# Sliding-window attention with sink keys feeding an MLP, on one core: the first four blocks' queries and keys read in 2,048-byte pieces, the sink values loaded early, a new written order

## The chip, the cores and the metric

The kernel runs on one core of one Trainium2 chip. The metric is the time of one execution in device microseconds (us); the kernel before was run three times. Engines are named as the profile names them: PE (matrix products), PEld (its weight loads), DVE (vector), ACT (activations), POOL, SP (both also start transfers; "POOLq" and "SPq" are their queues). PE reads from the on-chip working memory and writes to a small accumulator memory (PSUM), from which DVE and ACT copy results out.

## The reference

Two stages. Attention with batch 4, 8 heads, 768 positions and head size 64, where a query sees the last 128 positions and the first 4 (the sinks); then, per token, a two-layer MLP (512 to 2,048 to 512).

```python
scores = scale * np.matmul(q, k.transpose(0, 1, 3, 2))
is_sink = pos[None, :] < int(n_sink)                 # n_sink = 4
in_window = (rel >= 0) & (rel < int(window))         # window = 128, rel = query - key
scores = np.where(is_sink | in_window, scores, -1000000000.0)
a = softmax(scores); attn = a @ v
x = attn.transpose(0, 2, 1, 3).reshape(3072, 512)
h = x @ w_in                                         # 512 x 2048
out = (h * (1.0 / (1.0 + np.exp(-1.702 * h)))) @ w_out   # 2048 x 512
```

## The kernel before, in words

The 3,072 tokens are 24 blocks of 128 (six per batch). `ORDER` puts the four first blocks of the batches in front (0, 6, 12, 18): these see only themselves, so they need neither a previous block nor sinks. Two neighbouring places of `ORDER` form a group; the MLP runs over 12 groups of 256 tokens.

Per block: the queries, keys and values are loaded by POOL's queue with a cast from float32 to float16 (`load_block`, L273 for q and k, L254 for v). One load, the keys of the very first block, goes through SP's queue as float32 (`raw_k`, L261) and is cast by DVE (L269). Each of these loads puts a token on a partition and reads its 8 heads, that is, 128 x 8 pieces of 64 numbers, 256 bytes each. For the first eight blocks PE turns q and k (features onto partitions): four 128x128 transposes for q and four for k (L379, tile `tq`), copied to `qkT` by DVE or ACT (L344, L348). For later blocks a transposing transfer on SP does this (L401). Then scores `own` (and `prv` against the previous block, L449; `snk` against the sink keys, L478), a mask by DVE (L495), maximum (L505) and subtraction (L546), exponential on ACT (L585), transposition of the weights (by PE, L625, tile `ta`, for six blocks; by SP's queue, `at<-a`, for the rest), two selects on POOL (L588, L592), the product with v (`av`, L677 to L687), normalisation on DVE (L694, L695), a transposition (`tx`, L713, or SP's queue), and the MLP: `hT` = w_in by x (L748), the gate (ACT, L778; for the first group tanh on ACT, L762, and a product on DVE, L769), and `o` = gate by w_out (L802), copied to `osb` and stored.

The sink values take a path of their own. `vsa` is set to ones by DVE (L232), 4 rows of v per batch are loaded into it on SP (L318), a mask `ownm` is loaded on SP (L227), and POOL or DVE multiplies them into `vsb` (L323), which `av` reads for every block that has sinks (L677).

The order is written out: `SEQUENCE` lists all 834 steps with the engine that each is put on (`s` SP, `d` DVE, `t` POOL, `p` PE, `a` ACT), and each engine works through its own steps in this order. A step that waits holds up all that stands behind it on its engine. Numbers that the text uses: 0 is the load of the constants, 37 the `raw_k` load, 5 the setting of `vsa`, 93 to 96 the sink values' loads, 97 to 100 the `vsb` products, 21 to 26 the loads of w_in and v. The costs in `plan.add` served the search for the order; at run time they do nothing. Rings of buffers (`RING`) bound what may run ahead: three general PSUM tiles (`mm`), one `mi`, one `own`, one `pv`. POOL has at most eight loads under way: each further one waits for the load eight places before it.

Of the kernel before, what the change touches and what calls it, by code (L numbers as in the profile page):

```python
# [11 lines left out]
FP32 = mybir.dt.float32  # L12
# [7 lines left out]
P = 128  # L20
D = 64
# [16 lines left out]
    tanh=(0, 1),  # L38
    last=(256, 128, 128),
    hw=["k0"],  # L40
    avb={0: ("mi", "mm"), 1: ("mi", "mm"), 2: ("mi", "mm")},
    hb={},
    tqb={0: ("mm", "mi"), 1: ("mm", "mi")},
# [15 lines left out]
172p 21t 9d 7d 153p 134d 173a 30t 133d 136a 116p 29t 154d 175p 117a 156d 118p 24t 135a 139p 120p 158a 121d 137p 34t  # L59
138a 119d 140a 33t 155d 122p 176p 123a 157d 141p 143p 160p 142d 481p 159a 27t 144d 161a 177d 482a 145p 164p 484p  # L60
146a 483d 179d 485a 487p 28t 178d 486d 493p 488a 180d 162p 494a 489d 32t 163a 165d 490p 181a 495d 40t 166p 491a 478p
167d 128t 182a 492d 183p 479a 184d 36t 195p 480d 187p 185p 39t 193p 188d 499p 194a 186d 42t 189p 496p 500a 190d 105t
196a 501d 497a 168p 31t 198p 197p 169a 498d 215p 151t 191p 199d 217p 192a 514p 43t 218a 200d 502p 216a 515a 518p 48t
201d 203d 503p 202d 519a 508p 204a 49t 219p 509p 221d 35t 239p 510p 222d 240a 220p 504p 223d 44t 511p 224d 174t 505p
512a 225d 226a 45t 237p 520p 238d 5d 506a 93s 205p 241p 521a 206d 1s 242p 516p 243d 207t 530p 517a 244d 46t 524p 50t
245d 253p 525a 255p 531p 97t 254d 246d 256a 208p 52t 532p 247d 209d 54t 227p 257p 228a 522p 210t 259d 258p 230p 270s
533p 229t 260d 231a 523a 211p 261d 232t 528p 263d 212d 526p 529a 57t 262d 233p 527a 41t 536p 264a 234d 65t 537p 534d
55t 213p 271p 51t 214d 248a 235p 273d 538p 236a 249s 272p 539p 274d 548p 540a 265s 275d 556p 276d 549a 550p 296s
283p 557a 542p 285d 250t 551a 94s 552p 507s 543a 277d 286d 96s 544p 535s 61t 554p 545a 266t 553a 251p 555a 546p 252d
284p 564p 547a 287d 60t 278a 267p 288d 58t 565p 289d 47t 268d 558p 290a 100t 98d 269s 297p 559p 299d 279s 298p 560p  # L70
300d 566p 291s 301d 561p 303d 302d 322s 567p 562a 578p 304a 568d 280t 309p 579a 305s 580p 311d 310p 576p 563s 312d
292t 513s 572p 577a 581a 281p 570p 282d 67t 574p 313d 571a 53t 314d 293p 575a 66t 584p 573a 294d 306t 586p 585a 315d
295s 316a 582p 587p 70t 592p 62t 583a 317s 307p 56t 593p 308d 64t 588p 69t 323p 63t 598p 325d 72t 324p 594p 599a
326d 73t 589p 59t 327d 602p 590a 329d 328d 318t 595p 604p 596a 335p 605a 612p 337d 600p 613a 603a 348s 319p 606p
320d 608p 338d 607a 321s 601a 336p 610p 609a 339d 541s 330a 614p 341d 340d 615p 620p 342a 331s 621p 611a 616p 343s
361p 622p 597s 363d 374s 632p 364d 623p 633a 332t 362p 628p 365d 624d 617p 629a 366d 634p 75t 618a 636p 344t 619s
635a 349p 630p 351d 638p 84t 631a 367d 352d 345p 76t 639a 626p 79t 346d 350p 640p 71t 627a 353d 637a 333p 355d 78t
354d 641a 648p 68t 334d 356a 649p 347s 642p 375p 95s 368a 643p 377d 569s 376p 650p 357s 378d 644p 369s 379d 651p
380d 668p 591s 99t 400s 652d 645p 669a 85t 381d 656p 646d 358t 387p 647s 657a 664p 389d 666p 370t 390d 388p 662p
667a 391d 359p 663a 91t 658p 360d 81t 654p 393d 659a 392d 82t 665a 371p 655a 660p 74t 372d 670p 661a 373s 382a 401p  # L80
676p 403d 402p 671p 404d 394a 383s 677p 405d 672p 407d 395s 406d 678p 625s 673p 408a 413p 674a 409s 679p 415d 384t
684p 426s 680d 690p 685a 416d 696p 396t 385p 691a 688p 697a 386d 77t 414p 692p 689a 417d 87t 397p 418d 693a 682p 80t
419d 398d 686p 410t 683a 399s 698p 687a 420a 699p 88t 411p 86t 694p 412d 83t 421s 700p 695a 90t 427p 724p 429d 712p
725a 430d 428p 716p 713a 431d 720p 717a 432d 710p 433d 439p 711a 701p 721a 441d 422t 718p 702d 452s 704p 719a 442d
714p 653s 423p 715a 440p 434a 732p 424d 705p 443d 425s 444d 733p 435s 722p 445d 446a 706p 723a 447s 734p 707p 703s
675s 465p 708d 744p 467d 436t 752p 745a 468d 735p 753a 750p 92t 736a 437p 448t 751a 466p 740p 469d 438d 748p 741a
89t 471d 449p 470d 749a 738p 450d 746p 451s 453p 747a 726p 455d 742p 456d 454p 727p 743a 739a 457d 728p 472a 459d
458d 760p 729p 761p 460a 730d 772p 731s 473s 762p 773a 763p 709s 461s 770p 764a 774p 771a 768p 474t 775a 776p 769a
766p 777a 462t 780p 767a 778p 788p 779a 781a 475p 789p 476d 782p 463p 754p 464d 783p 477s 755p 681s 784p 785p 756p
786a 790p 787s 802p 791p 803a 757p 792a 794p 804p 758a 795a 759s 808p 805a 793s 796p 737s 809a 765s 800p 797a 806p  # L90
801a 798p 807a 810p 799a 822p 811p 823p 812p 816p 813p 824p 814a 817p 825p 818p 815s 826d 828p 827s 819p 829p 820d
830p 831p 821s 832a 833a
"""


# [69 lines left out]
def kernel(  # L165
# [50 lines left out]


    def hw(key, cost, fn, xfer, **kw):
        return plan.add(SP, key, cost, fn, xfer=xfer, post=1.3, **kw)

    def by(e):
        return nc.sync if e == SP else nc.scalar
# [26 lines left out]
    def load_block(which, b, key, after=0.0):  # L249
        bb, r = divmod(b, 6)  # L250
        pair, i = divmod(PLACE[b], 2)
        src = {"q": q, "k": k, "v": v}[which][bb, :, r * P : (r + 1) * P, :].rearrange("h s d -> s h d")
        if which == "v":
            return sw(key, 0.88, lambda b=b, x=2: nc.gpsimd.dma_start(v65[:, b, :, 0:D], src), 0.93 if pair < 4 else 1.05, deps=[z_1], after=after)  # L254
        w = "qk".index(which)
        buf = qkn[pair]
        if which + str(PLACE[b]) in CFG["hw"]:
            raw = const.tile([P, H, D], FP32, name=f"raw_{which}{b}")
            n = CFG["hw"].index(which + str(PLACE[b]))
            got = plan.add(  # L260
                {SP: 0.45, ACT: 0.6}, -120 + n, 0, lambda e, src=src, raw=raw, x=9: by(e).dma_start(raw, src), xfer=1.2, post=0.6  # L261
            )

            def round16(e, b=b, w=w, i=i):
                dst, src = buf()[:, i, w], raw
# [94 lines left out]
    for p, b in enumerate(ORDER):  # L360
# [8 lines left out]
        if p in CFG["tq"]:  # L369
            tps = [ps(t, (P, 4, P), FP16, f"tq{b}_{w}") for w, t in enumerate(CFG["tqb"][p])] if p in CFG["tqb"] else []  # L370
            tps = tps or [ps("mm", (P, 8, P), FP16, f"tq{b}")] * 2

            def tp(w, tps=tps):
                return tps[w]()[:, 4 * w : 4 * w + 4] if tps[0] is tps[1] else tps[w]()

            def t_qk(w, g=g, i=i, tp=tp):
                src = qkn[g]()[:, i, w].rearrange("p h d -> p (h d)")
                for c in range(4):
                    nc.tensor.transpose(tp(w)[:, c], src[:, bass.ts(c, P)], ident)  # L379

            def copy_qk(e, w, b=b, p=p, tp=tp):
                copy(e, qk_of(b)[:, 4 * w : 4 * w + 4], tp(w))

            parts = []
            for w in range(2):
                a = plan.add(
                    PE, K0 - 48 + w, 0.24, lambda w=w, f=t_qk: f(w), deps=[ld["qk"[w] + str(b)], o_const],
                    take=[tps[w]], give=[qkn[g]],
                )
                parts.append(  # L390
                    plan.add(
                        {DVE: 0.34, ACT: 0.5}, K0 - 48 + w, 0,
                        lambda e, b=b, w=w, f=copy_qk: f(e, w),
                        deps=[a], take=[qkt[g]], give=[tps[w]],
                    )
                )
            o_qkt[b] = parts
        elif i == 0:

            def t_qk(g=g):  # L400
# [3 lines left out]

            o_qkt[b] = o_qkt[ORDER[p + 1]] = [
                plan.add(
                    SP, K0 - 48, 1.4, t_qk, deps=[ld[f"{w}{n}"] for w in "qk" for n in ORDER[p : p + 2]], take=[qkt[g]],
                    give=[qkn[g]], xfer=2.56, post=0.75,
                )
            ]  # L410
# [452 lines left out]
```

## Time and profile before

| | |
|---|---|
| median of three runs | 229.97 us (229.97 to 230.83) |
| the profiled execution: its own time | 231.84 us |
| its span, first to last instruction | 230.1 us |
| busy: PE, DVE, ACT, POOL | 215.8, 132.7, 130.5, 117.5 us |
| first MLP product (`hT`) starts at | 19.33 us |
| last PE instruction ends at about | 227 us |
| pieces moved by POOL's queue | 78,064 |

The profile shows one execution. A row of a table by windows gives, for a stretch of the span, each engine's busy time and its count of instructions, the granted clock, the share of the 16 transfer engines (it can pass 1 where transfers overlap) and GB/s, counted at the destination. A row of a list of waits gives the waiting engine and line, what ended the wait, the total, how often, and the longest. A row of the timeline gives start, length, engine, line, what is written from what, and in brackets how long the engine stood idle before it and what ended that.

### The profile page before, as it was taken

The numbers are of one execution on the slowest core, as the hardware profiler recorded it, in microseconds if no ns is written. First come the engines' busy times: TensorE is split into PE (matmuls) and PEld (weight loads), VectorE is DVE, ScalarE is ACT, GpSimd is POOL, SyncE is SP. The second block draws the span as 40 slices with busy tenths as digits, with TensorE's granted clock in tenths as the row PEclk, the third lists the DMA queues.
The fourth block names the chain that finished last, engine by engine and source line by source line (L and its number), as shares of the span: only waits on it lengthen the run. The fifth ranks groups of instructions, "written<-read, shape, count | busy, mean of one in ns | idle before, by whom it ended". The sixth has DMA issues, their size and how long they took to land.

```text
span 230.1 us, 5428 instructions
## 1 busy us (share of the span) xinstructions
PE 215.8 (94%) x2282; PEld 151.8 (66%) x2282; DVE 132.7 (58%) x236; ACT 130.5 (57%) x188; POOL 117.5 (51%) x138
## 2 busy tenths in 40 slices
PE   1796899998999999999999999999999999999994
PEld 0555785777685586576686586596866865855864
DVE  3579887778858863556566877672873672030001
ACT  2388679644867268247558338659555538512621
POOL 8974574569639279950493573497213700700000
PEclk9999999999999999999999999999999999999999
DMA  9999999999999999999999899899999544304402
GB/s 114 146 178 206 168 207 187 154 74 140 96 147 201 169 179 169 124 140 165 240 142 132 180 169 161 181 162 126 114 124 238 37 59 106 90 3 137 182 3 91
DMA packets 130680, 32.47 MB, mean 141 GB/s; under 512 B 123072, under 2 KB 127712, under 8 KB 130656
## 3 DMA queue, kind: packets, MB, share of 16 engines
q0 software_dynamic: 78064, 13.51, 82.0%
q1 hardware_dynamic: 52448, 18.55, 42.4%
q8 instruction: 18, 0.29, 0.5%
q10 hardware_dynamic: 144, 0.07, 0.1%
q14 instruction: 6, 0.05, 0.1%
HBM read 27.46 MB, written 6.29 MB: 147 GB/s over the span
## 4 chain that ended last, share of the span: by engine, by line
PE 69%; DMA 14%; POOL 12%; SPq 1%; issue 1%; DVE 1%; ACT 1%; POOLq 0%
PE o L802 30%; PE hT L748 28%; DMA w_in<-in_moe_w_in_dram 5%; POOL qkn L273 5%; DMA at<-a 5%; DMA v<-in_v_dram 2%; PE own L449 2%; DMA ownm<-cown 2%; PE av L683 2%; POOL atp L588 2%; POOL at L592 2%; PE av L687 2%; POOL v L254 2%; PE prv L449 1%; PE av L677 1%; SPq L650 1%
## 5 line engine op out<-in xcount | busy, mean ns | idle before, releaser
L748 PE MATMUL hT<-xT,w_in 128*128 128x256 f16 (+1 forms) x896 | 93.6, 257 | 1.7 <-DMA w_in<-in_moe_w_in_dram 1.3
L802 PE MATMUL o<-w_out,gT 128*128 128x512 f16 (+2 forms) x416 | 90.5, 363 | 0.0
L748 PEld LDWEIGHTS <-w_in 128*128 128x128 f16 x896 | 75.3, 98 | 14.3 <-DMA w_in<-in_moe_w_in_dram 2.0
L778 ACT ACTIVATE gT<-hT 128x512 f16<-128x512 f32 x88 | 50.7, 597 | 52.8 <-PE hT L748 52.7
L802 PEld LDWEIGHTS <-gT 128*128 128x128 f16 x416 | 37.2, 98 | 33.9 <-ACT gT L778 0.3
L588 POOL TENSOR_SCALAR_AFFINE_SELECT atp<-at 128x1024 f16<-128x1024 f16 (+1 forms) x22 | 22.3, 1014 | 60.2 <-DMA at<-a 46.6
L495 DVE COPY_PREDICATED own<-consts,prv 128x1024 f32<-128x1024 uint16 x20 | 24.6, 1229 | 22.8 <-PE prv L449 22.7
L505 DVE TENSOR_REDUCE mx<-own 128x8 f32<-128x1024 f32 (+1 forms) x28 | 29.8, 1069 | 3.5 <-PE own L449 3.0
L546 DVE TENSOR_TENSOR e<-own,mx 128x1024 f32<-128x1024 f32 (+1 forms) x28 | 29.7, 1064 | 0.8
L585 ACT ACTIVATE a<-e 128x1056 f16<-128x1056 f32 (+1 forms) x28 | 26.0, 952 | 2.6 <-issue 1.8
L273 POOL DMA_DIRECT2D qkn<-in_k_dram x23 | 20.9, 910 | 4.4 <-DMA w_out<-in_moe_w_out_dram 2.1
L592 POOL TENSOR_SCALAR_AFFINE_SELECT at<-at 128x1024 f16<-128x1024 f16 (+1 forms) x22 | 22.2, 1010 | 1.5
L273 POOL DMA_DIRECT2D qkn<-in_q_dram x24 | 21.6, 906 | 2.7 <-DMA w_out<-in_moe_w_out_dram 1.9
L254 POOL DMA_DIRECT2D v<-in_v_dram x24 | 21.6, 904 | 1.5 <-DMA w_out<-in_moe_w_out_dram 1.2
L694 DVE RECIPROCAL rcp<-av 128x8 f32<-128x8 f32 (+1 forms) x28 | 5.5, 197 | 28.8 <-PE av L687 28.1
L344 DVE COPY osb<-o 128x512 f32<-128x512 f32 (+2 forms) x11 | 6.9, 627 | 25.3 <-PE o L802 25.3
L348 ACT COPY osb<-o 128x512 f32<-128x512 f32 (+1 forms) x13 | 7.3, 561 | 21.8 <-PE o L802 21.8
L683 PE MATMUL av<-v,at 128*128 128x65 f16 x192 | 16.9, 194 | 1.7 <-POOL at L592 1.0
L695 DVE TENSOR_TENSOR xn<-av,rcp 128x512 f16<-128x512 f32 (+1 forms) x28 | 17.2, 616 | 1.0
L683 PEld LDWEIGHTS <-at 128*128 128x128 f16 x192 | 13.9, 98 | 3.5 <-POOL at L592 2.0
L449 PEld LDWEIGHTS <-qkT 64*128 64x128 f16 x352 | 10.3, 96 | 7.0 <-issue 5.5
L687 PE MATMUL av<-v,atp 128*128 128x65 f16 x160 | 14.7, 194 | 0.0
(49 smaller groups left out, 168.9 us busy)
## 6 DMA issues: line engine op xcount, KB each, us to landing
out_dram<-osb SPq DMA_DIRECT2D x23, 256.0 KB, 2.5
qkn<-in_q_dram POOLq DMA_DIRECT2D x24, 128.0 KB, 6.0
v<-in_v_dram POOLq DMA_DIRECT2D x24, 128.0 KB, 5.0
qkn<-in_k_dram POOLq DMA_DIRECT2D x23, 128.0 KB, 4.7
w_in<-in_moe_w_in_dram POOLq DMA_DIRECT2D x4, 512.0 KB, 10.7
w_out<-in_moe_w_out_dram POOLq DMA_DIRECT2D x4, 512.0 KB, 11.6
at<-a SPq DMA_TRANSPOSE x18, 4.9
raw_k<-in_k_dram SPq DMA_DIRECT2D x1, 256.0 KB
```

What stands on the lines that cost most here:

```text
L254: return sw(key, 0.88, lambda b=b, x=2: nc.gpsimd.dma_start(v65[:, b, :, 0:D], src), 0.93 if pair < 4 else 1.05, deps=[z_1], after=after)
L273: key, 0.88, lambda b=b, w=w, i=i: nc.gpsimd.dma_start(buf()[:, i, w], src), 0.93 if pair < 4 else 1.05,
L495: nc.vector.copy_predicated(out=own(lo, hi).rearrange("p l j s -> p (l j) s"), mask=later.unsqueeze(1).to_broadcast((P, 4 * (hi - lo), P)) ...
L505: lambda lo=lo, hi=hi, own=half, small=small: nc.vector.tensor_reduce(out=small[:, lo:hi], in_=own(lo, hi), axis=AX.X, op=ALU.max),
L546: nc.vector.tensor_tensor(out=e32()[:, 512 * lo : 512 * hi].rearrange("p (l j s) -> p l j s", j=4, s=P), in0=own(lo, hi), in1=small[:, lo: ...
L585: nc.scalar.activation(out=a16()[:, lo:hi], in_=e32()[:, lo:hi], func=AF.Exp, scale=scale)
L588: nc.gpsimd.affine_select(out=atp()[:, lo : lo + n], in_=at()[:, lo : lo + n], pattern=[[0, n], [-1, P]], compare_op=ALU.is_gt, fill=0.0, ...
L592: nc.gpsimd.affine_select(out=at()[:, lo : lo + n], in_=at()[:, lo : lo + n], pattern=[[0, n], [1, P]], compare_op=ALU.is_ge, fill=0.0, ba ...
L683: nc.tensor.matmul(acc[:, j], at()[:, c], v65[:, b, h], start=(r == 0), stop=(r == 0))
L748: nc.tensor.matmul(ht()[:, n], w_in16[:, c, bass.ts(f, P)], xt[g]()[:, tok, c], start=(c == 0), stop=(c == 3))
L778: lambda fs=fs, cols=cols, gt=gt, ht=ht: nc.scalar.activation(out=gt()[:, fs[0] : fs[-1] + 1, cols], in_=ht(), func=AF.Gelu_apprx_sigmoid),
L802: nc.tensor.matmul(po(), gt()[:, F, bass.ts(t, P)], w_out16[:, F, cols], start=(F == 0), stop=(F == NF - 1))
```

## The change

For the four blocks in front (`big`), q and k are no longer read token by token. A partition now takes one head and eight neighbouring tokens (16 token groups x 8 heads = 128 partitions), so that each of its reads is 8 x 64 numbers in a row, 2,048 bytes, and a load has 128 pieces where it had 1,024. Turning such a tile takes 16 products per tile in place of four: for each of the eight tokens in a partition and each parity of the head, 64 columns of the tile are multiplied with 64 columns picked out of the identity, into one half of the PSUM partitions, in float32. The copy to `qkT` puts the tokens back in order by strides, and reads float32 in place of float16. For blocks 2 and 3 of `ORDER`, q and k now each take a whole `mm` tile where they shared one.

The constants are loaded ahead of `raw_k`. The setting of `vsa` and two of the four sink loads come at the start, the other two later, together. `SEQUENCE` is new throughout, since it was searched again with other costs and with a limit on pieces under way; the first line shows the manner.

```diff
-37s 10d 4d 0s 12t 2d 3d 11a 13t 14t 6d 38d 15t 106p 17t 101p 16t 103p 102d 124p 19t 104d 107p 18t 126p 109d 147p 20t
-127a 108d 148a 22t 125a 110d 149p 23t 170p 8d 111d 150a 129p 130p 112a 25t 152p 113a 131d 114p 26t 171a 132d 115a
...
+0s 6d 37s 10d 7d 12t 5d 4d 93s 11a 14t 3d 94s 13t 1s 106p 38d 23t 2d 103p 15t 101p 104d 16t 126p 102a 19t 107p 127d
+18t 8d 124p 109d 20t 147p 125a 108d 17t 148a 129p 110d 130p 22t 111d 112a 149p 131d 25t 150a 172p 132d 113a 105t
...
+            raw = const.tile([P, H * D], FP32, name=f"raw_{which}{b}")
+            src = {"q": q, "k": k}[which][bb, :, r * P : (r + 1) * P, :].rearrange("h (t e) d -> h t (e d)", e=8)
...
+        if PLACE[b] in CFG["big"]:
+            return sw(
+                key, 0.8,
+                lambda b=b, w=w, i=i: nc.gpsimd.dma_start(
+                    buf()[:, i, w].rearrange("p h d -> p (h d)"),
+                    {"q": q, "k": k}["qk"[w]][bb, :, r * P : (r + 1) * P, :].rearrange("h (t e) d -> h t (e d)", e=8),
+                ),
+                0.7, take=[buf], after=after,
+            )
...
+            if p in CFG["big"]:
+                tps = [
+                    ps(t, (P, 4, P), FP32, f"tq{b}_{w}")
+                    for w, t in enumerate(CFG["tqb"].get(p, ("mm", "mm")))
+                ]
...
+                if p in CFG["big"]:
+                    dst = tp(w).rearrange("p c t -> p (c t)")
+                    for e in range(8):
+                        for a in range(2):
+                            nc.tensor.matmul(
+                                dst[64 * a : 64 * a + 64, 64 * e : 64 * e + 64],
+                                src[:, 64 * e : 64 * e + 64],
+                                ident.rearrange("p (c a t) -> p c a t", a=2, t=16)[:, :, a], start=True, stop=True,
+                            )
+                    return
...
+                if p in CFG["big"]:
+                    dst, src = (
+                        dst.rearrange("p c (t e) -> p c t e", e=8),
+                        src.rearrange("p x y -> p (x y)").rearrange("p (e c t) -> p c t e", c=4, t=16),
+                    )
```

More of the change, by code (lines that the diff above doesn't have):

```diff
@@ L40 @@
     hw=["k0"],
+    big=(0, 1, 2, 3),
     avb={0: ("mi", "mm"), 1: ("mi", "mm"), 2: ("mi", "mm")},
@@ L62 @@
[L62 to L71, printed above, removed]
@@ new lines @@
+680a 414p 690p 685a 416d 681s 396t 696p 409s 417d 385p 697a 426s 692p 691a 386d 682p 418d 693a 397p 683a 410t 686p
+398d 688p 419d 687a 399s 694p 689a 87t 420a 698p 80t 411p 88t 699p 412d 89t 695a 421s 700p 90t 712p 83t 427p 713a
+92t 718p 429d 86t 428p 710p 719a 430d 720p 711a 431d 701p 721a 432d 724p 422t 439p 725a 714p 702a 441d 452s 704p
+715a 442d 423p 716p 424d 705p 653s 433d 717a 425s 434a 440p 706p 443d 444d 732p 722p 445d 446a 435s 707p 723a 733p
+447s 465p 734p 708a 467d 742p 675s 468d 735p 436t 744p 736a 466p 738p 745a 448t 750p 739a 743a 437p 751a 746p 438d
@@ L93 @@
+830p 821a 831p 832a 833a
 """
@@ L218, in hw @@
     def hw(key, cost, fn, xfer, **kw):
-        return plan.add(SP, key, cost, fn, xfer=xfer, post=1.3, **kw)
+        return plan.add(SP, key, cost, fn, xfer=xfer, post=6.0, **kw)
     def by(e):
@@ L257, in load_block @@
         if which + str(PLACE[b]) in CFG["hw"]:
-            raw = const.tile([P, H, D], FP32, name=f"raw_{which}{b}")
+            raw = const.tile([P, H * D], FP32, name=f"raw_{which}{b}")
             n = CFG["hw"].index(which + str(PLACE[b]))
+            src = {"q": q, "k": k}[which][bb, :, r * P : (r + 1) * P, :].rearrange("h (t e) d -> h t (e d)", e=8)
             got = plan.add(
-                {SP: 0.45, ACT: 0.6}, -120 + n, 0, lambda e, src=src, raw=raw, x=9: by(e).dma_start(raw, src), xfer=1.2, post=0.6
+                {SP: 0.45, ACT: 0.6}, -120 + n, 0, lambda e, src=src, raw=raw, x=9: by(e).dma_start(raw, src), xfer=0.75, post=0.6
             )
             def round16(e, b=b, w=w, i=i):
-                dst, src = buf()[:, i, w], raw
+                dst, src = buf()[:, i, w].rearrange("p h d -> p (h d)"), raw
                 if e == ACT:
@@ L381, in copy_qk @@
             def copy_qk(e, w, b=b, p=p, tp=tp):
-                copy(e, qk_of(b)[:, 4 * w : 4 * w + 4], tp(w))
+                dst, src = qk_of(b)[:, 4 * w : 4 * w + 4], tp(w)
+                if p in CFG["big"]:
[3 more added lines that the diff above has]
+                    )
+                copy(e, dst, src)
             parts = []
@@ L386 @@
                 a = plan.add(
-                    PE, K0 - 48 + w, 0.24, lambda w=w, f=t_qk: f(w), deps=[ld["qk"[w] + str(b)], o_const],
+                    PE, K0 - 48 + w, 0.43 if p in CFG["big"] else 0.24, lambda w=w, f=t_qk: f(w), deps=[ld["qk"[w] + str(b)], o_const],
                     take=[tps[w]], give=[qkn[g]],
@@ L391 @@
                     plan.add(
-                        {DVE: 0.34, ACT: 0.5}, K0 - 48 + w, 0,
+                        {DVE: 0.6 if p in CFG["big"] else 0.34, ACT: 0.5}, K0 - 48 + w, 0,
                         lambda e, b=b, w=w, f=copy_qk: f(e, w),
@@ L406 @@
                 plan.add(
-                    SP, K0 - 48, 1.4, t_qk, deps=[ld[f"{w}{n}"] for w in "qk" for n in ORDER[p : p + 2]], take=[qkt[g]],
+                    SP, K0 - 48, 1.75, t_qk, deps=[ld[f"{w}{n}"] for w in "qk" for n in ORDER[p : p + 2]], take=[qkt[g]],
                     give=[qkn[g]], xfer=2.56, post=0.75,
```

54 lines of the change are left out of this document (29 added, 25 removed).

## The prediction

> **What bounds the kernel now.** I read the page first, then PE's busy time by windows, the waits of PE, SP and POOL, and the timeline of the first 30 us.
>
> The page, sections 1 to 3: PE's total, its slices, POOL's queue.
>
> ```profile
> PE 215.8 (94%) x2282; PEld 151.8 (66%) x2282; DVE 132.7 (58%) x236; ACT 130.5 (57%) x188; POOL 117.5 (51%) x138
> PE   1796899998999999999999999999999999999994
> q0 software_dynamic: 78064, 13.51, 82.0%
> ```
>
> PE is full except at both ends. So the time is PE's work plus PE's idle time, and the change can win only idle time or lose by added work. The windows say where the idle is (second column: length; third: PE busy):
>
> ```profile
> 4.00:8.00 4.00, 3.00 (x22) 1.70 (x22) 1.25 (x3) 0.00 (x0) 4.00 (x6) 1.00 2.16 138
> 8.00:12.00 4.00, 2.64 (x20) 1.68 (x18) 2.60 (x5) 2.40 (x5) 4.00 (x6) 1.00 2.37 149
> 16.00:20.00 4.00, 3.11 (x55) 2.42 (x53) 3.83 (x11) 3.72 (x8) 1.76 (x2) 1.00 1.28 205
> 20.00:24.00 4.00, 2.48 (x44) 2.17 (x42) 3.97 (x9) 2.24 (x5) 1.22 (x2) 1.00 1.40 198
> 24.00:28.00 4.00, 3.62 (x66) 3.39 (x64) 2.87 (x8) 3.23 (x6) 1.99 (x4) 1.00 2.27 161
> 50.00:60.00 10.00, 9.36 (x150) 7.07 (x148) 7.68 (x15) 5.76 (x9) 9.71 (x13) 1.00 1.18 105
> 70.00:80.00 10.00, 9.57 (x83) 4.97 (x82) 8.99 (x17) 4.97 (x6) 5.94 (x6) 1.00 1.39 174
> 90.00:100.00 10.00, 9.48 (x85) 5.56 (x84) 4.94 (x8) 4.37 (x7) 9.48 (x11) 1.00 2.58 125
> ```
>
> Between 20 and 28 us PE stands 1.52 + 0.38 = 1.90 us; from 50 to 100 us 0.64 + 0.43 + 0.52, with 0.12 between 60 and 70 us: 1.71 us. The waits name the causes:
>
> ```profile
> PE hT L748 <- DMA w_in<-in_moe_w_in_dram: 1.3, 1, 1.3
> PE av L683 <- POOL at L592: 0.6, 1, 0.6
> POOL vsb L323 <- DMA vsa<-in_v_dram: 5.4, 1, 5.4
> POOL vsb L323 <- DMA ownm<-cown: 1.9, 1, 1.9
> SPq L318 <- DVE at L344: 43.0, 1, 43.0
> ```
>
> SP waits 43 us at its first sink load, since the setting of `vsa` stands late on DVE; POOL then waits for the sinks at `vsb`, with the selects that `av` needs queued behind. For prices, the timeline:
>
> ```profile
> 10.61 1.03 PE L379 MATMUL tq<-consts,qkn 128*128 128x128 f16 x8 [1.26 <-DMA qkn<-in_k_dram]
> 29.14 0.39 PE L379 MATMUL tq<-consts,qkn 128*128 128x128 f16 x4
> 18.85 0.42 PE L683 MATMUL av<-v,at 128*128 128x65 f16 x8
> 23.30 1.96 PE L748 MATMUL hT<-xT,w_in 128*128 128x128 f16 x32 [1.26 <-DMA w_in<-in_moe_w_in_dram]
> 25.86 0.90 PEld L748 LDWEIGHTS <-w_in 128*128 128x128 f16 x16 [0.55 <-DMA w_in<-in_moe_w_in_dram]
> ```
>
> **The loads.** In the windows 4 to 12 us POOL's queue moves 138 to 149 GB/s in 256-byte pieces: a q or k load (131 KB written) takes 0.88 to 0.95 us. The last two w_in pieces, already read 2,048 bytes at a time, let PE go on at 23.30 and 25.86 us: 524 KB in 2.56 us, 205 GB/s. At that rate a q or k load takes 0.64 us, 0.25 less; seven of them stand ahead of w_in: 1.75 us. (Bounds: nothing, if something other than the pieces sets the rate; 7 x 0.6 = 4.2 us if the load costs only its share of pieces.) In the new order the same ten q, k and v loads precede the last two w_in pieces, with v2 moved ahead of the first. So the last two land at about 21.5 and 24.1 us, the first 1.75 - 0.9 = 0.85 us earlier. POOL's own issue (0.9 us for a small-piece load, 0.75 us for a w_in load with half as many pieces) can only get shorter; at 0.9 it would still keep ahead of a queue that is backed up to 26 us.
>
> **The first block's chain.** The constants' load goes first: `raw_k` starts at 1.32 instead of 0.81 us. At its present 3.16 us to landing that is 4.48 us; cast (0.43) to 4.9. Then a tile is turned by 16 products instead of four. No row has a product of 64x64. Lower bound: 65 columns in `av`, (0.42 - 0.19) / 7 = 0.033 us each. That is a late row; early, eight 128-column transposes take 1.03 us, (1.03 - 0.31) / 7 = 0.103 us apart, later four take 0.39, (0.39 - 0.22) / 3 = 0.057. The early pace is 1.8 times slower. So 16 cost at least 16 x 0.033 x 1.8 = 0.95 us early, at most 16 x 0.103 = 1.65 us if a narrow product is no cheaper than a wide one; four cost 0.41 now. The nearest row in columns is the 65, so 0.95: +0.54 us a tile. The copy from float32 is priced by L505 and L546, which read 128x512 float32 from PSUM in 0.68 us; on DVE 0.42 becomes 0.68 (two copies, as now; twice that if strides hurt, nothing at best); on ACT it stays 0.59, since L348 takes 0.56 to 0.59 us from float32 as from float16.
>
> Walked in the new order: keys turned 4.9 to 6.05, copied to 6.75; the next key tile waits for that copy (its `mi` tile is single), and the first scores queue behind it on PE: 7.9 instead of 7.49 us. Then it goes faster. Now ACT takes four copies and waits for the third block's keys before the first exponential at 11.74 us; in the new order only three copies precede it: about 10.9. PE then has a mask, scores and two tiles (0.95 each) before the first `ta`, about 13.4 as now (13.38). First `av` 14.6 instead of 16.20, but the last q tile and a second block's `av` come before `tx`. I get the first `hT` at 19.0 to 19.5 and take it as unmoved (19.33).
>
> So eight tiles add 8 x 0.54 = 4.3 us of PE work, all before the first `hT`, where PE stood 4.3 us for the constants and, by the waits and windows, 2.5 us more between 6 and 20 us. The cover is that idle time and the wait for w_in; with it gone, each tile would cost its 0.54 in full. What the loads win is the wait at 23.30 (1.3 us) and part of what follows it: of 1.90 us idle I take 1.4. Next in line are DVE, busy 3.97 of 4 us between 20 and 24, and the four w_out pieces; the new order takes the products that need the second to fourth of these a little later, which fits.
>
> **The sinks.** DVE's setting (0.28 us) and two SP issues (0.73 us each) go ahead of SP's first transposing transfer, which began at 51.09 us: free. They pass nothing on SP except `ownm`. On DVE all the settings before the cast add up to some 1.7 us from 0.88, done before 4.48. On POOL the first `vsb` (1.12 us) now stands at about 14 us, ahead of loads that wait for a place among eight anyway. Gone are POOL's waits of 1.9 and 5.4 us, with them the 0.6 us of PE at 54 us and perhaps the 0.43 near 75. The third, 0.52 at 92 us, is a v load, and the new order leaves the v load of the sixth place hardly more PE work ahead of its use than this one had. I take 0.6 of 1.71 us. Bounds: -1.7, and +2 if the new order waits twice as much as the old.
>
> **The sum.** -1.4 - 0.6 = -2.0 us. The profiled execution took 231.84 us (230.1 and 1.74 around it), 1.87 above the median; so 229.8 on its account and 228.0 as the median.
>
> **The rivals.** No change that can be told is 0.5%, 1.15 us: 228.8 to 231.1.
>
> Narrow products at the price of wide ones (slower). At 0.103 us a pair a tile takes 1.65 us, +1.24. Seven tiles stand before the first `ta`: 8.7 us, less the 7 x 0.54 = 3.8 already walked: first `hT` 4.9 us later than walked, partly made up as PE's pace quickens and as all of w_in then waits ready: +2.5 us, 232.5. It decides from about 0.075 us a pair. For it: no row with 64 columns of weights. Against: the 65-column row. The Trainium skill, TensorEngine Tiling (Array Packing), section Restrictions, says that column tiling switches the fast weight load off, and TensorE: Matmul & The Clock Gate, section LDWEIGHTS, gives a load as columns / 1.2 ns, an estimate of 53 ns for 64; by these a tile takes 0.85 us at the late pace and 1.5 at the early one, which is this rival. No row of before shows such a load.
>
> The loads gain nothing (no change). The read's outermost dimension is now 8 heads instead of 128 tokens; if that spreads a load over half the transfer engines, a lone 131 KB takes 1.28 us instead of 0.64, `raw_k` lands about 1 us later, and only overlapped loads regain it. Then only the sinks' 0.6 is left: 229.4. For it: the two `qkn` waits between 8 and 11 us show that latency counts. Against: the queue is backed up, so two halves can work at once. The Trainium skill, DMA: Bandwidth & Descriptors, in the paragraph How many engines (k), states exactly this choice of engines from the slowest dimensions of both sides; no run here shows it yet.
>
> The new order brings waits (slower). Attention for blocks 4 and 5 or a v load comes late; one select behind one transposing transfer is worth 1 to 3 us: 231.5. For it: every lead is new. Against: the shortest lead of a full block's select before its `av` is now two MLP steps of PE (0.87 us each) and a scores step, where it was two MLP steps.
>
> More than forecast: the first `hT` 1 us earlier and all waits after 50 us gone: -3.7 us, 226.3.
>
> **How the numbers follow.** Forecast (227 to 228.8) 0.41; more 0.15; nothing from loads 0.18; narrow products dear 0.13; waits 0.13. Faster is the first two plus a little of the third, 0.57; same 0.17; slower 0.26. The range leaves out the ends of the extremes: 226.0 to 231.8; the forecast's own is 227.0 to 228.8.
>
> **What would show it.** Right: the last two w_in pieces landing near 21.5 and 24.1 us, no PE wait above 0.5 us after 20, `tq` products near 0.06 us apart early, first `hT` near 19.3, SP's first sink load near 2 us, no POOL wait for `vsa`. Wrong: `tq` pairs 0.1 us apart, `raw_k` landing after 5.5 us, or PE idle above 2 us beyond 30.

## The result and the profile after

The changed kernel takes 233.47 us (median of 20 runs, 230.84 to 235.56), the kernel before on the same chip 230.72 (20 runs, 229.78 to 232.12). The ratio is 1.0089, with a 95% interval of 1.0064 to 1.0114: slower by 0.9%, where 228.0 was forecast. The ratio leaves out six slow runs of the changed kernel (234.61 us and above), so it is lower than that of the two medians, 1.0119. The profiled execution took 233.78 us with a span of 232.1, against 231.84 and 230.1 before.

The page of the changed kernel, sections 1 to 3, the lines that were shown of before:

```profile
PE 214.7 (92%) x2378; PEld 151.8 (65%) x2378; DVE 136.8 (59%) x243; ACT 133.7 (58%) x187; POOL 115.5 (50%) x136
PE   1579999999999899998899999998999999999994
q0 software_dynamic: 72688, 13.51, 76.2%
```

PE's busy time is 1.1 us less (214.7 for 215.8 us), so its idle time within the span is 3.1 us more. The second row has new dips in the 14th, 19th, 20th and 28th of the 40 slices (5.8 us each: about 75 to 81, 104 to 116 and 157 to 162 us), and one of before's, in the 10th (52 us), no longer stands out. The windows give their size. The changed kernel (columns: stretch, length, then busy time and count of PE, PEld, DVE, ACT, POOL, the granted clock, the transfer engines' share, GB/s):

```profile
0.00:28.00 28.00, 18.52 (x334) 13.95 (x335) 20.16 (x48) 15.92 (x29) 20.61 (x33) 1.00 1.41 165
28.00:50.00 22.00, 21.40 (x285) 15.48 (x284) 17.66 (x33) 17.08 (x24) 12.22 (x16) 1.00 1.72 167
50.00:70.00 20.00, 19.47 (x252) 14.81 (x251) 17.09 (x28) 12.81 (x18) 17.44 (x21) 1.00 1.62 151
70.00:100.00 30.00, 29.26 (x295) 20.00 (x295) 18.82 (x31) 20.42 (x25) 16.06 (x19) 1.00 1.33 154
100.00:120.00 20.00, 18.18 (x195) 12.17 (x193) 12.49 (x20) 10.26 (x14) 10.13 (x11) 1.00 1.20 165
150.00:180.00 30.00, 28.86 (x307) 20.97 (x305) 17.07 (x29) 20.10 (x27) 14.61 (x15) 1.00 1.39 148
```

The kernel before, by the same stretches:

```profile
28.00:50.00 22.00, 21.73 (x281) 15.60 (x280) 17.86 (x35) 15.87 (x24) 12.96 (x22) 1.00 1.68 165
50.00:70.00 20.00, 19.23 (x256) 14.77 (x254) 14.18 (x23) 12.46 (x19) 14.14 (x18) 1.00 1.35 126
70.00:100.00 30.00, 29.05 (x290) 18.93 (x289) 20.25 (x35) 16.35 (x21) 23.55 (x25) 1.00 1.73 163
100.00:120.00 20.00, 20.00 (x202) 14.26 (x200) 11.00 (x17) 12.00 (x17) 9.06 (x10) 1.00 1.67 179
150.00:180.00 30.00, 30.00 (x315) 21.70 (x313) 17.68 (x30) 18.69 (x26) 15.52 (x17) 1.00 1.14 144
```

Length less PE's busy time is its idle time. From 28 to 220 us the changed kernel stands idle 0.60 + 0.53 + 0.74 + 1.82 + 1.14 = 4.83 us; the kernel before stood 1.99 (0.27, 0.77 and 0.95 in the first three, nothing behind 100 us). That is 2.84 us more; what is new, 1.82 and 1.14 us, lies behind 100 us, where PE had been full. This sum, "idle beyond 28 us", is the yardstick for the experiments below.

The start is a little better. The timeline of the changed kernel:

```profile
7.58 0.43 DVE L271 CAST qkn<-raw_k 128x512 f16<-128x512 f32 x1 [4.31 <-DMA raw_k<-in_k_dram]
8.07 1.06 PE L398 MATMUL tq<-consts,qkn 128*64 128x64 f16 x32 [4.06 <-DVE qkn L271]
17.09 0.44 PE L398 MATMUL tq<-consts,qkn 128*64 128x64 f16 x16
19.23 1.06 PE L780 MATMUL hT<-xT,w_in 128*128 128x128 f16 x16
22.22 0.89 POOL L284 DMA_DIRECT2D qkn<-in_q_dram  x1 [1.78 <-DMA w_in<-in_moe_w_in_dram]
24.80 0.88 POOL L284 DMA_DIRECT2D qkn<-in_k_dram  x1 [1.70 <-DMA w_in<-in_moe_w_in_dram]
32.94 1.02 PE L834 MATMUL o<-w_out,gT 128*128 128x512 f16 x4
```

The same rows of the kernel before:

```profile
23.54 0.74 POOL L291 DMA_DIRECT2D w_out<-in_moe_w_out_dram  x1 [1.79 <-DMA w_in<-in_moe_w_in_dram]
26.10 0.74 POOL L291 DMA_DIRECT2D w_out<-in_moe_w_out_dram  x1 [1.82 <-DMA w_in<-in_moe_w_in_dram]
34.12 1.03 PE L802 MATMUL o<-w_out,gT 128*128 128x512 f16 x4
```

The first product of the second MLP layer, `o`, starts at 32.94 us, where before it started at 34.12: 1.2 us won. Less 1.2 and plus 2.84 makes 1.6 of the 2.0 us of span. The two POOL rows are loads that wait until a w_in load gives its queue place back; in the kernel before the loads that waited so began 1.3 us later, so w_in lands 1.3 us earlier. And the keys are late: the cast at 7.58 us still waited for `raw_k`, 6.4 us after its issue at 1.21; before it was 3.97, 3.2 us after its issue at 0.81.

The waits of PE in the changed kernel (what waited, for what: total, times, longest):

```profile
PE tq L398 <- DVE qkn L271: 4.1, 1, 4.1
PE own L473 <- DMA consts<-cconst: 3.0, 1, 3.0
PE own L481 <- DMA qkT<-qkn: 1.7, 1, 1.7
PE av L715 <- DVE at L355: 1.2, 1, 1.2
PE hT L780 <- DMA xT<-xn: 1.1, 1, 1.1
PE own L481 <- DVE e L578: 0.6, 1, 0.6
PE av L715 <- DMA v<-in_v_dram: 0.5, 1, 0.5
PE o L834 <- DMA w_out<-in_moe_w_out_dram: 0.4, 1, 0.4
```

The wait for w_in (1.3 us) is gone, as is the 0.6 us for a select at 54 us. New behind the start are, above all, `own` for `qkT`, 1.7 us, and `hT` for `xT`, 1.1 us. Two pieces of the timeline of the changed kernel say where they come from:

```profile
98.69 1.09 POOL L620 TENSOR_SCALAR_AFFINE_SELECT atp<-at 128x1024 f16<-128x1024 f16 x1 [5.53 <-PE hT L780]
99.85 1.09 POOL L624 TENSOR_SCALAR_AFFINE_SELECT at<-at 128x1024 f16<-128x1024 f16 x1
100.89 0.89 POOL L284 DMA_DIRECT2D qkn<-in_k_dram  x1
104.30 3.60 SPq L433 DMA_TRANSPOSE qkT<-qkn  x1
111.37 0.40 PE L481 MATMUL own<-qkT 64*128 64x128 f16 x8 [1.71 <-DMA qkT<-qkn]
...
156.18 1.23 SPq L758 DMA_TRANSPOSE xT<-xn  x1
162.25 1.05 PE L780 MATMUL hT<-xT,w_in 128*128 128x256 f16 x8 [1.15 <-DMA xT<-xn]
```

In the first, POOL issues a key load only after two selects, ahead of the first of which it stood idle for 5.53 us. SP, whose queue carries the transposing transfer of these keys, waits for the load until 104.30 us. The transfer lands 7.0 us later, by the chain that ended last, and PE has waited 1.71 us for it. In the second, an `xT` transfer takes 6.0 us to land; their median in this execution is 3.3. Slow transfers alone do not make such waits: in the kernel before one `xT` transfer took 6.3 us (median 3.3), and no `hT` waited for it.

### The profile page after: what moved, and what is told of

The parts are those of the page before. It is cut to its first block, busy times and chain, and to the rows that moved or that the text cites. A ratio compares the mean times of both kernels' runs of the same rounds, so it can differ in the third digit from the quotient of the medians.

```text
span 232.1 us, 5621 instructions
## 1 busy us (share of the span) xinstructions
PE 214.7 (92%) x2378; PEld 151.8 (65%) x2378; DVE 136.8 (59%) x243; ACT 133.7 (58%) x187; POOL 115.5 (50%) x136
## 4 chain that ended last, share of the span: by engine, by line
PE 61%; DMA 23%; DVE 7%; POOL 6%; issue 1%; ACT 0%; POOLq 0%; DVEq 0%
PE hT L780 26%; PE o L834 26%; DMA w_out<-in_moe_w_out_dram 6%; DMA qkn<-in_k_dram 5%; DMA v<-in_v_dram 4%; DMA qkT<-qkn 3%; DMA qkn<-in_q_dram 3%; DMA xT<-xn 3%; PE own L481 2%; PE av L715 2%; PE av L719 2%; DVE own L527 2%; DVE mx L537 2%; PE av L709 2%; PE prv L481 2%; POOL w_in L293 1%
## 5 line engine op out<-in xcount | busy, mean ns | idle before, releaser
L834 PE MATMUL o<-w_out,gT 128*128 128x512 f16 (+2 forms) x416 | 91.6, 363 | 0.6 <-DMA w_out<-in_moe_w_out_dram 0.4
L284 POOL DMA_DIRECT2D qkn<-in_q_dram x20 | 17.8, 897 | 4.9 <-DMA w_out<-in_moe_w_out_dram 3.1
L284 POOL DMA_DIRECT2D qkn<-in_k_dram x20 | 17.7, 889 | 4.3 <-DMA w_in<-in_moe_w_in_dram 1.7
L355 DVE COPY osb<-o 128x512 f32<-128x512 f32 (+1 forms) x11 | 7.2, 651 | 20.1 <-PE o L834 20.1
L359 ACT COPY osb<-o 128x512 f32<-128x512 f32 (+2 forms) x13 | 7.0, 542 | 19.4 <-PE o L834 17.7
```

What stands on the lines that cost most here:

```text
L834: nc.tensor.matmul(po(), gt()[:, F, bass.ts(t, P)], w_out16[:, F, cols], start=(F == 0), stop=(F == NF - 1))
```

## The experiments

Each ratio is to the kernel before on the same chip, whose medians there were 230.97 to 231.31 us, with its 95% interval; it can differ by 0.3% from the quotient of the medians. A kernel's profile is that of one execution of it. The theory after the result was that the order behind the start makes the loss, and the wide pieces and the new start do not. The rivals were that the wide loads make it themselves, by late keys and by what they collide with, and that the moved sinks do.

**The new loads in the old order.** All of the change but the order: `SEQUENCE` is that of the kernel before.

```diff
-0s 6d 37s 10d 7d 12t 5d 4d 93s 11a 14t 3d 94s 13t 1s 106p 38d 23t 2d 103p 15t 101p 104d 16t 126p
+37s 10d 4d 0s 12t 2d 3d 11a 13t 14t 6d 38d 15t 106p 17t 101p 16t 103p 102d 124p 19t 104d 107p 18t
...
```

> The changed loads and turning products with the old written order. Theory 1 (the new order's waits cost the time, the loads themselves win a little): no slower than before, 228.5 to 230.5 us, PE idle beyond 28 us below 2.2 us. Theory 2 (the new loads cost the time: keys in raw_k late, float32 copies): slower by 1 us or more, 231.5 to 233.5, with the idle time ahead of 28 us.

**The old loads in the new order.** The kernel before, with the changed kernel's `SEQUENCE` alone (the same two lines the other way round).

> The loads and transposes of before with the new written order (sinks early included). Theory 1: slower than before, 231.5 to 234 us, PE idle beyond 28 us 4 us or more as in the changed kernel (4.8). Theory 2: as before or faster, 229 to 230.7 us.

Measured: new loads in the old order 229.79 us, 0.9978 (0.9950 to 1.0007), no difference that can be told; old loads in the new order 231.94 us, 1.0044 (1.0019 to 1.0069), slower. The order alone makes about half of the loss of 0.9%; its idle time beyond 28 us, 1.60 us, is far below the 4 us that were expected with it. The wide loads cost nothing that can be told in the old order; in the new one the whole change stands at 1.0089 against 1.0044 without them, and these two intervals just overlap.

**One key load earlier.** In the changed kernel step 67, the key load of the row at 100.89 us, moves ahead of step 318 (the two selects at 98.69 and 99.85 us) and of two other POOL steps, loads. In the old order it stood ahead of 318.

```diff
-308d 63t 595p 59t 323p 596a 62t 604p 325d 587p 605a 326d 602p 318t 598p 603a 324p 606p 599a 327d 328d 588p 67t 607a
+308d 63t 67t 595p 59t 323p 596a 62t 604p 325d 587p 605a 326d 602p 318t 598p 603a 324p 606p 599a 327d 328d 588p 607a
```

> The changed kernel with one step moved: POOL's load of the keys that the transposing transfer at 104 us waits for goes ahead of the select that it stood behind. If that in-order wait is a cause (theory 1), PE's wait of 1.7 us at 111 us goes and the time falls by 1 to 1.7 us; if the waits beyond 28 us only replace each other or come from transfer rates, the time stays within 0.5 us of the changed kernel.

Measured: 231.47 us, 1.0029 (1.0001 to 1.0056). Its interval lies wholly below that of the changed kernel: one step's place is worth 1.0089 - 1.0029 = 0.6%, 1.4 us. In its timeline SP's transfer goes out 4.8 us earlier, and no `own` waits for `qkT` any more; by windows PE's idle time from 100 to 120 us falls from 1.82 to 0.19 us (this execution took 230.17 us, 1.3 less than the median, but that of the last experiment, which makes the same move and took 232.07, has 0.19 too):

```profile
99.51 1.77 SPq L439 DMA_TRANSPOSE qkT<-qkn  x1
```

```profile
100.00:120.00 20.00, 19.81 (x215) 14.24 (x213) 14.29 (x26) 11.01 (x16) 11.90 (x14) 1.00 1.24 173
```

The place alone does not make the wait: in the profile of the old loads in the new order the two steps stand the same way, and `own` waits only 0.2 us for `qkT`. The chain of the changed kernel puts the transfer's start down to the v load that POOL issues after the keys; with the key load moved, the transfer goes out at 99.51 us, ahead of that v load (100.20), so it waited for the keys.

**The new start with the old rest.** The changed kernel through the first 209 entries of its order, to the step 505; behind them all steps that are left, in the order of the kernel before.

```diff
 ... 242p 511p 521a 46t 241p 512d 505p
-243d 55t 516p 506a 244d 524p 517a 245d
+151t 35t 44t 174t 506a 205p 206d 516p
...
```

> The changed kernel with the new order up to the last second-layer product of the first block (about 41 us) and the old order behind it. Theory 1: keeps the 1.2 us won at the first second-layer product and the old order's small waits: 228 to 229.7 us. Theory 2: slower than before, 231 us or more.

**The same order with the old loads.** The kernel before with that joined order.

> The loads and transposes of before, with the new order up to the first block's last second-layer product and the old order behind it. If the wide pieces earn what the hybrid with them wins (0.9945): 0.997 to 1.001 of before. If the order and the early sinks earn it: 0.993 to 0.996.

Measured: with the new loads 229.25 us, 0.9945 (0.9921 to 0.9969); with the old loads 229.24 us, 0.9931 (0.9896 to 0.9965). Both beat the kernel before, and from 50 to 220 us PE is full. The kernel with the new loads, by windows:

```profile
100.00:120.00 20.00, 20.00 (x217) 14.57 (x215) 12.73 (x23) 12.00 (x18) 10.41 (x11) 1.00 1.11 166
150.00:180.00 30.00, 30.00 (x317) 21.68 (x315) 17.80 (x32) 18.62 (x25) 15.80 (x17) 1.00 1.01 127
```

The first `hT` and the first `o` with the old loads:

```profile
17.59 1.06 PE L754 MATMUL hT<-xT,w_in 128*128 128x128 f16 x16
32.78 1.02 PE L808 MATMUL o<-w_out,gT 128*128 128x512 f16 x4
```

With the runs so far there is a table of loads against order (ratio to the kernel before; idle beyond 28 us in the profile):

| order | old loads | new loads |
|---|---|---|
| old | 1 (1.99 us) | 0.9978 (2.26 us) |
| new start, old rest | 0.9931 (0.21 us) | 0.9945 (0.22 us) |
| new | 1.0044 (1.60 us) | 1.0089 (4.83 us) |

Down each column, from the second row to the third, only the order behind the start differs: with the new loads 1.0089 / 0.9945 = 1.4%, or 3.3 us; with the old ones 1.1%, or 2.6 us. Neither pair of intervals overlaps, and this settles where the loss is. (The profiled execution of the old loads in the new order took 230.82 us, 1.1 less than their median, so its 1.60 us may be less than is usual.) Along each row only the loads differ, and in the two upper rows they make no difference that can be told.

The profiles show one more thing that goes with the order behind the start. From issue to landing, the slowest `qkT` transfer takes 9.1 to 10.4 us in all seven kernels with the new order behind the start, later experiments included (9.4 in the changed one), and 5.2 to 8.2 in the seven with the old one (7.5 in the kernel before). So the new order also has slower transfers at the worst; what slows them, and what that costs, is not shown.

**The sinks alone.** The kernel before, with only the setting of `vsa` (5), two of the four sink loads (93, 94), the load of the mask (1) and one product (97) moved to the start.

```diff
-37s 10d 4d 0s 12t 2d 3d 11a
+37s 10d 4d 0s 12t 5d 93s 1s 94s 2d 3d 11a
...
-118p 24t
+118p 24t 97t
...
```

> The kernel before with only the setting of vsa, two sink loads, the mask's load and the first vsb product moved to the start. If the sink wait cost PE time (as forecast, 0.6 us): POOL's waits for vsa and ownm near 50 us go, PE's 0.6 us at 54 us goes, 0.3 to 1 us faster. If it was hidden behind other work: within 0.3 us of before.

**The new order with the sinks late.** The changed kernel, with the sinks' steps put back near where the kernel before had them.

```diff
-0s 6d 37s 10d 7d 12t 5d 4d 93s 11a 14t 3d 94s 13t 1s 106p
+0s 6d 37s 10d 7d 12t 4d 11a 14t 3d 13t 106p
...
+238a 5d 503p
...
+506a 93s 244d
...
```

> The changed kernel with the setting of vsa, the sink loads, the mask's load and the first vsb product put back to where the old order has them. If the early sinks are worth about 1.5 us in this order too, as in the old one: 1.014 to 1.019 of before, with POOL's waits for vsa and ownm back. If the new order hides them: 1.006 to 1.011.

Measured: the sinks alone give 229.39 us, 0.9932 (0.9899 to 0.9966), which is 0.8 to 2.3 us won. That is as much as the whole new start brings with the old rest (0.9931 and 0.9945), so nothing else in that start is shown to gain. The profile has 0.66 us less idle beyond 28 us, from 50 to 70 us 0.77 less, and the first `o` 0.64 us earlier (33.48), for which no row names a cause; profiles of one start with the same loads differ by as much. POOL's two waits at `vsb` turn out to be two different ones. In the kernel before:

```profile
50.08 1.12 POOL L323 TENSOR_TENSOR vsb<-vsa,ownm 32x520 f16<-32x520 f32 x1 [1.95 <-DMA ownm<-cown]
128.41 1.12 POOL L323 TENSOR_TENSOR vsb<-vsa,ownm 32x520 f16<-32x520 f32 x1 [5.37 <-DMA vsa<-in_v_dram]
```

With the sinks alone early the one at 50 us is gone, and the long one stays:

```profile
126.27 1.12 POOL L329 TENSOR_TENSOR vsb<-vsa,ownm 32x520 f16<-32x520 f32 x1 [5.45 <-DMA vsa<-in_v_dram]
```

In both profiles PE is full from 120 to 150 us, so the long wait costs nothing there.

In the new order putting the sinks back late gives 233.10 us, 1.0102 (1.0058 to 1.0146), not to be told from 1.0089. POOL then waits 5.3 us for `vsa` again, but at 73 us, and not at the first `vsb` (49.23 us), whose load went out at 36.70 us where the kernel before had it at 44.11; so this run does not bring back the wait at 50 us. The early sinks do not make the loss, since late ones win nothing. Whether the gain that they bring in the old order is hidden in the new one, this run does not settle.

**Tokens outermost.** In the changed kernel's reads and `raw_k` the 16 token groups become the outer dimension and the 8 heads the inner one. The pieces stay at 2,048 bytes. The identity's columns are picked to match.

```diff
-.rearrange("h (t e) d -> h t (e d)", e=8)
+.rearrange("h (t e) d -> t h (e d)", e=8)
...
-ident.rearrange("p (c a t) -> p c a t", a=2, t=16)[:, :, a], start=True, stop=True,
+ident.rearrange("p (t c a) -> p c t a", c=4, a=2)[:, :, :, a], start=True, stop=True,
```

> The changed kernel, but a load's partitions run tokens first, heads within (16 token groups outermost in the read in place of 8 heads; same 2,048-byte pieces, the identity's columns picked to match). If the outermost 8 is what makes the keys in raw_k land 6.4 us after their issue (theory A), they land within 3.2 to 4.2 us, the cast starts by 5.4 us in place of 7.6, the first hT falls below 18.5 us and the time falls by 0.7 to 2 us against the changed kernel. If they are late for another reason, what is queued around them or the longer issue of 0.86 us (theory B), the cast stays at 7 us or later and the time within 0.5 us.

**The same with the old rest.**

> The same reading order with the new order up to the first block's last second-layer product and the old order behind it. Theory A: 0.7 to 2 us below the same hybrid with heads outermost (0.9945 of before): 0.987 to 0.992 of before. Theory B: 0.993 to 0.996.

Measured: 233.83 us, 1.0120 (1.0066 to 1.0175), and with the old rest 228.80 us, 0.9909 (0.9879 to 0.9938). Neither can be told from its like with 8 heads outermost (1.0089 and 0.9945), and the gain that was expected did not come in the new order. The timeline of the first of the two:

```profile
5.68 0.46 DVE L271 CAST qkn<-raw_k 128x512 f16<-128x512 f32 x1 [2.40 <-DMA raw_k<-in_k_dram]
6.19 3.03 PE L398 MATMUL tq<-consts,qkn 128*64 128x64 f16 x48 [2.24 <-DVE qkn L271]
16.85 1.10 PE L398 MATMUL tq<-consts,qkn 128*64 128x64 f16 x16
```

The keys are cast 1.9 us earlier, so the order of the reads' dimensions sets when they land. The busy share of the 16 transfer engines from 0 to 8 us, in slices of 0.2 us, first of the changed kernel, then of this one:

```profile
DMA  0000000015882184563355579679999999999999
DMA  0000000005861492398999999999999999999999
```

With 8 outermost it stands at three to six tenths from 3.0 to 4.6 us, while `raw_k` and several of POOL's loads are under way, and stays at nine only from 5.4 us; with 16 outermost it does so from 3.8 us. But the products now lie (3.03 - 0.19) / 47 = 0.060 us apart early and (1.10 - 0.19) / 15 = 0.061 late (0.19 for the last one, as `av` has it), where the changed kernel has 0.028 and 0.017. The columns picked from the identity are now eight elements apart, where they were runs of 16. The first `hT` is at 19.63 us: what the keys won, the products lost.

**Tokens outermost, columns side by side.** The picked identity is loaded as 128 further columns of the constants, so that a product reads 64 neighbouring columns.

```diff
+    pick = np.array([8 * t + 2 * c + a for a in range(2) for c in range(4) for t in range(16)])
...
+    identp = consts[:, 4 * P + 4 : 5 * P + 4].bitcast(FP16)
...
-                                ident.rearrange("p (t c a) -> p c t a", c=4, a=2)[:, :, :, a], start=True, stop=True,
+                                identp[:, 64 * a : 64 * a + 64], start=True, stop=True,
```

> The changed kernel with tokens outermost in the first blocks' reads, as before, but the identity's columns laid out in the constants in the order in which they are used, so that each product reads 64 neighbouring columns. If the eighth-column reads made the products slow in the first try (0.062 us apart against 0.027), they are 0.027 us or less apart again; raw_k's cast again near 5.7 us, so the first hT falls to 17 to 18.3 us. The time: 0.5 to 2 us below the changed kernel, 1.000 to 1.007 of before. If the early keys do not matter, 1.007 to 1.012.

**The same with the old rest.**

> The same with the new order up to the first block's last second-layer product and the old order behind it. If early keys carry through to the end: 0.984 to 0.991 of before; if w_in or DVE takes over as the limit at the start: 0.991 to 0.995, as the hybrids with other loads.

Measured: in the new order 232.71 us, 1.0055 (1.0017 to 1.0094); with the old rest 227.72 us, 0.9857 (0.9815 to 0.9898), the fastest of all, below both kernels. The timeline of the second:

```profile
6.08 0.48 DVE L280 CAST qkn<-raw_k 128x512 f16<-128x512 f32 x1 [2.80 <-DMA raw_k<-in_k_dram]
6.62 1.06 PE L407 MATMUL tq<-consts,qkn 128*64 128x64 f16 x32 [2.46 <-DVE qkn L280]
18.75 1.06 PE L789 MATMUL hT<-xT,w_in 128*128 128x128 f16 x16
32.45 1.02 PE L843 MATMUL o<-w_out,gT 128*128 128x512 f16 x4
```

The quick products are back, with the keys cast at 6.08 us. Against the new start with the old rest (0.9945) these two edits are worth 0.9%, 2 us, and the intervals do not overlap; the profiles place the first `o` 0.7 us earlier (32.45 for 33.13), which is a part of that. In the new order the same two edits (1.0055) cannot be told from the changed kernel. The price of the order behind the start is there again: 1.0055 / 0.9857 = 2.0%, or 4.6 us.

**The second wait as well.** The key load earlier, and on PE the steps 701 and 427 ahead of 712, which gives `xT` more PE work ahead of its use.

```diff
-421s 700p 90t 712p 83t 427p 713a 92t 718p 429d 86t 428p 710p 719a 430d 720p 711a 431d 701p 721a
+421s 700p 90t 701p 427p 712p 83t 713a 92t 718p 429d 86t 428p 710p 719a 430d 720p 711a 431d 721a
```

> The changed kernel with the key load moved up as in the earlier run and, on PE, one second-layer step and one scores step put ahead of the first-layer step that waited 1.1 us at 162 us for its transposed input. If named waits in the new order are the loss: another 0.5 to 1 us, 0.997 to 1.001 of before, PE idle beyond 28 us below 1 us. If such waits only move on to the next step: as the key load alone, 1.003.

Measured: 231.23 us, 1.0000 (0.9971 to 1.0030). In its profile, PE's waits for `qkT` are gone and that for `xT` is at 0.2, but idle beyond 28 us is 2.71 us, where below 1 was expected, and others stand there that the changed kernel had smaller or not at all:

```profile
PE o L840 <- ACT gT L816: 1.0, 2, 0.8
PE av L721 <- DMA v<-in_v_dram: 0.9, 1, 0.9
```

The interval overlaps that of the key load alone, so the second move is not shown to help. From here to the new start with the old rest (0.9945) there is still 0.55%, 1.3 us. No one wait accounts for it, and the profiles name different ones. That remainder is settled as the new order's, not step by step. That the eight loads which POOL issues beside the slow `xT` transfer at 156 us delay it was only argued, from 6.0 us to landing against 3.3; it was not tried.

## Why the prediction was wrong

**The step that failed** is the term for the waits behind the start: "I take 0.6 of 1.71 us. Bounds: -1.7, and +2 if the new order waits twice as much as the old." The profile shows 2.84 us more idle where 0.6 less was forecast, and the sign that was named, PE idle above 2 us beyond 30, came true. The new idle time, 1.82 and 1.14 us, lies at two waits behind 100 us that the kernel before does not have, and the table of loads against order puts 1.1 to 1.4%, 2.6 to 3.3 us, on the order behind the start. The rival "the new order brings waits" is what happened, though not quite by the mechanism that it named: it had a select behind a transposing transfer, and what came was a key load behind two selects, with the transposing transfer behind the load, 1.4 us by the run that moves the load. It had a chance of 0.13 and 231.5 us; the time was 233.47, since more than one place lost. Its argument against, that the shortest lead of a select before its `av` had not shrunk, looked at a kind of lead that held: no `av` of the changed kernel waits for a select. The lead that broke is that of a load before the transposing transfer that needs it, and of that transfer before its scores. The first could be read in the written order: 67 stands behind 318. The upper bound was too low too: a new order has no tie to the waits of the old one, so twice the old idle time was no bound at all. Of the 5.5 us between 228.0 and 233.47, 0.75 belongs to the kernel before, taken at 229.97 and measured at 230.72.

**The loads.** "So the last two land at about 21.5 and 24.1 us", 1.75 us earlier: 1.3 measured, but with another order at the start. Where only the loads differ, the loads that wait for w_in begin 1.77 and 1.73 us earlier in the old order (21.77 and 24.37 for 23.54 and 26.10 us), as worked out, and 0.3 to 1.2 us earlier with the new start (22.22 and 24.80 for 22.51 and 25.06 with the old rest, or 23.38 and 25.93 in the new order). So the pieces do help a backed-up queue, and PE's wait for w_in is gone. But the gain on the time that hung on it is not shown to come from the pieces. With the same new start and the old loads the first `o` is at 32.78 us, in spite of 1.4 us of waits for w_in, because the first `hT` is already at 17.59 (18.23 in the new order's profile). With the new loads it is at 33.13, and the ratios do not differ. (Profiles of kernels with the same start and the same loads place the first `o` up to 0.9 us apart, so only the ratios carry this.) What the pieces win at w_in, they give back at the keys.

**The keys.** "At its present 3.16 us to landing that is 4.48 us; cast (0.43) to 4.9": the cast began at 7.58. This sign of a wrong forecast was named (landing after 5.5 us) and came true, and it is part of the rival "the loads gain nothing": the outermost dimension of the read was 8. With 16 outermost, the same bytes in the same pieces land 4.4 to 4.9 us after the issue, in four profiles, where they took 6.4 to 7.1, in five. The Trainium skill, DMA: Bandwidth & Descriptors, in the paragraph How many engines (k), lets the slowest dimensions of both sides choose the number of transfer engines, up to 16; by it the reads with 8 heads outermost use half the engines. The landing times and the busy share of the engines agree in sign, and no view here shows which engines carried a load. Even the better read is later than the small pieces, which took 3.2 us, and 3.3 with the new start. The rival's "about 1 us later" was a third of the 3.2 us measured; in the old order, with `raw_k` issued first, it was 1.6 us.

**The narrow products.** 0.95 us was taken for 16 early, between 0.95 and 1.65. Measured: 32 in 1.06 us, little more than half of the lower bound, and late 16 in 0.44. The rival of dear narrow products is refuted for this layout; the estimate from the Trainium skill for a load of 64 columns (TensorE: Matmul & The Clock Gate, section LDWEIGHTS: 53 ns) is above the 28 and 17 ns from product to product. The price of the copies from float32 held: 0.69 us on DVE and 0.59 on ACT, where 0.68 and 0.59 were taken.

**The first `hT`.** "19.0 to 19.5" was forecast and 19.23 measured, but through two errors that cancel: keys 3.1 us later than the walk had them, and products at half price. An agreement of the sum is no proof of its terms: with the keys cast at 6.04 and 6.08 us and the products as quick, the first `hT` stands at 17.76 and 18.75 us (tokens outermost, columns side by side, new order and old rest).

**The start's gain.** 1.4 us was taken and 1.2 seen at the first `o`; by the runs the new start with the old rest is 0.55% or 1.3 us better in all, sinks included.

**The sinks.** SP's first sink load at 2.12 us, the first `vsb` at 14.07, no wait of POOL for `vsa`: as forecast. But the prediction read the waits of 1.9 and 5.4 us as one cause, and the second lay at 128 us, where PE was full. Alone the sinks are worth 1.6 us (0.8 to 2.3), more than the 0.6 taken; the profile accounts for 0.66 us of it behind 28 us. In the new order the wait at 54 us gave way to 0.53 us for a v load at 56.

## What to carry to other kernels

When a change brings new loads and a newly searched order at once, price the order as a part of its own: the old order behind the changed part was the cheapest good version here, and it beat the searched one by 1.4%. In a written order, check the lead of every load ahead of the transposing transfer that reads it, and of that transfer ahead of its use, against landing times as measured (in the changed kernel 3.0 to 6.0 us for `xT`, 4.3 to 9.4 for `qkT`), and ask what stands ahead of the load on its engine. For reads with long pieces, try a dimension of 16 in place of 8 outermost, and let products read neighbouring columns: together they were worth 0.9% here, with the old rest.

## What the runs showed of the hardware

- Products with 64 columns of weights that go in turn to the two halves of the PSUM partitions lie 0.028 us apart early and 0.017 late, where 128-column transposes lie 0.103 apart early. Half of that would be 0.052; why they lie closer still, no row shows.
- The same products with moving columns eight elements apart take 0.060 us each, early and late alike.
- The same 256 KB in the same 2,048-byte pieces land after 6.4 to 7.1 us with 8 outermost and after 4.4 to 4.9 with 16 outermost, behind the load of the constants. With 8 outermost and issued first, they took 4.8 us.
- Transposing transfers of `xT` in one execution of the changed kernel landed after 3.0 to 6.0 us, in one of the kernel before after 3.0 to 6.3; those of `qkT` after 4.3 to 9.4 and 4.5 to 7.5.
